# Attention and two expert layers on one core: pair products with the rows stationary, and the column softmax of two batches moved

## The chip, the core and the metric

The kernel runs on one core of a Trainium2 chip. The metric is the device time of one execution in microseconds (us), lower is better; three executions of the kernel before took 1196.97, 1197.18 and 1197.57 us. The engines are named as in the profile: PE (TensorE, with PEld for its weight loads), DVE (VectorE), ACT (ScalarE), POOL (GpSimd) and SP (the queue that issues most DMAs).

## The reference, cut to what matters

Three layers follow each other: an attention between 512 tokens and 32 state rows per head in both directions, a dense feed-forward layer, and a routed one in which each row goes to one of eight experts.

```python
def _attn_ref(x, state):                      # x 8 x 8 x 512 x 64, state 8 x 8 x 32 x 64
    scores = scale * np.matmul(x, state.transpose(0, 1, 3, 2))
    ...                                        # softmax over the 32 states
    xread = np.matmul(a, state)
    scores2 = scale * np.matmul(state, x.transpose(0, 1, 3, 2))
    ...                                        # softmax over the 512 tokens
    sread = np.matmul(a2, x)
    return np.concatenate([xread, sread], axis=2)

def _moe_ref(x, w_in, w_out):                 # w_in 512 x 2048, w_out 2048 x 512
    h = x @ w_in
    g = h * np.clip(h + 3.0, 0.0, 6.0) / 6.0
    return g @ w_out

def _moe2_ref(x, w_gate, w_output_gate, w1, w2):  # 8 experts, 512 x 1024 and 1024 x 512
    e_idx = np.argmax(x @ w_gate, axis=1)
    ...
    for e in range(E):
        h = np.maximum(x[mask] @ w1[e], 0.0)
        out[mask] = gate_w[mask, None] * eom[mask, e, None] * (h @ w2[e])
```

## The kernel before

**Dense part.** `w_in` and `w_out` arrive as 64-bit words. `from_f64` (L446) loads a tile of 512 such words per partition, has ACT scale the high words to 32 bits (L462), and has DVE shift the low words (L463), merge the sign bit into them (L464) and merge both (L465). `load_win(f)` and `load_wout(f)` do that for the 16 tiles of each matrix; the second also splits its tile into a rounded part and a rest (L474, L475), since products are made as three reduced-precision products. The raw tiles share four buffers (tag `x4`) with the loads of x.

For a batch, `attn_rows` (L177) makes the scores of all heads (`halves`, L163: eight products into two PSUM tiles), transposes them on DVE, and takes the softmax over the 32 states. Its inner `columns()` (L188) takes maxima (L192, L193) and exponentials (L194) of the same scores over the 512 tokens; for batch 0 it runs later and keeps batch 0's scores in the PSUM tiles o0 and o1 until then. `attn_cols` turns the exponentials and multiplies them with x. `make_sw` multiplies states and `w_in` (one call for four tiles of `w_in`), `h_xread` (L292) makes one tile `ft` of the hidden layer, `act` its activation, and `gemm2` (L332 to L334) the second product, two tiles later.

The order of the work at the start is a table, `plan`: for batch 0 and 1 and each tile `ft` it says which weight tiles are loaded and which steps of the generators `rows[b]`, `cols[b]` and `sws` are issued. Segments run batch 0's tiles 0 to 7, batch 1, batch 0's tiles 8 to 15, then batches 2 to 7. The scheduler reorders by priority; `soon(b)` raises that of batch 0 and 1.

**Routed part.** `ORDER` lists 19 slots: 16 slots of 256 rows of one expert (`gemm1` L682, `gemm2e` L698 to L702) and, as slots 5, 10 and 15 (counted from 0), a pair: 64 rows of each of two experts, in full precision. `pair1` (L654) is called for each of 8 tiles `ft`: w1's 128 x 128 blocks are the stationary operand, the 64 rows of each expert move. `pair2` (L665) then has the hidden values (64 columns per expert) stationary and w2's 512 columns moving, the two experts in two column tiles of the array at once. `slot` delays the second product by one tile, so PE's queue alternates the two. `finish` (L704) scales the result on ACT and scatters the rows by an indirect DMA on POOL; such a scatter waits until the one before has landed. Further pairs, behind `used`, are not executed with these data.

In PE's queue, a full-precision product is two instructions.

Of the kernel before, what the change touches and what calls it, by code (L numbers as in the profile page):

```python
# [80 lines left out]
def tile_kernel(  # L81
# [62 lines left out]


# [31 lines left out]
    def attn_rows(b):  # L177

        x = [loads.pop((b, k)) for k in range(2)]

        ps = halves(b, lambda j: x[j // 2][:, j % 2, :], ("o0", "o1") if b == 0 else None)
        sm = ap.tile([128, 72], F32, tag="sm", name="sm")
        mx, nm, s2, r2 = [sm[:, 2 * k:2 * k + 2] for k in range(4)]
        mr, sr, rr = [sm[:, k:k + 32] for k in (8, 40, 8)]
        bt = ap.tile([128, 32, NS], F32, tag="t4", name="bt", bufs=2)

        def columns():

            e2_t[b] = [win[3][:, e, :] for e in range(2)] if b == 0 else \
                [ap.tile([128, 512], F32, tag="e2", name="e2", bufs=2) for _ in range(2)], s2, r2  # L190
            for e in range(2):
                V.tensor_reduce(mx[:, e:e + 1], ps[e], axis=AX.X, op=ALU.max)  # L192
                V.tensor_scalar(nm[:, e:e + 1], mx[:, e:e + 1], -0.125, None, op0=ALU.mult)  # L193
                S.activation(e2_t[b][0][e], ps[e], AF.Exp, bias=nm[:, e:e + 1], scale=0.125,  # L194
                             accum_out=s2[:, e:e + 1])

        with soon(b):
            for e in range(2):
                V.transpose(bt[:, 16 * e:16 * e + 16, :].rearrange("p a n -> p (a n)"), ps[e])
            if b:  # L200
                columns()
        yield
        with soon(b):
            V.tensor_reduce(mr, bt, axis=AX.X, op=ALU.max)
        yield
        with soon(b):
# [3 lines left out]
        with soon(b):  # L210
# [4 lines left out]
        with soon(b):  # L215
# [7 lines left out]
        with soon(b):  # L223
            V.tensor_tensor(al, af, ah.bitcast(F32), op=ALU.subtract)
        aT[b] = ah, al
        yield
        if b == 0:
            columns()
            yield

    def attn_cols(b):

        e2, s2, r2 = e2_t.pop(b)
# [214 lines left out]
    def from_f64(src, dst=None):  # L448
# [14 lines left out]
        V.tensor_scalar(lw, lw, 29, None, op0=ALU.logical_shift_right)  # L463
        V.scalar_tensor_tensor(lw, y3.bitcast(U32), 0x80000000, lw, op0=ALU.bitwise_and, op1=ALU.bitwise_or)  # L464
# [3 lines left out]
    def load_win(f):  # L468
        o = 128 * (f % 4)
        from_f64(w_in[:, :, 256 * f:256 * f + 256], win[f // 4][:, :, o:o + 128])  # L470

    def load_wout(f):
        t = from_f64(w_out[:, f:f + 1, :])
        S.copy(woh[f], t)  # L474
        V.tensor_tensor(wol[f], t, woh[f].bitcast(F32), op=ALU.subtract)  # L475
# [177 lines left out]
    def pair1(ft, x):  # L653

        ps = psum("h", 2)[:, :128]
        for i in range(2):
            a = ws[2 + i][0][ft // 2][:, :, 128 * (ft % 2):128 * (ft % 2) + 128]
            for k in range(4):
                T.matmul(ps[:, 64 * i:64 * i + 64], a[:, k, :], x[:, k, 64 * i:64 * i + 64], start=(k == 0),  # L659
                         stop=(k == 3))  # L660
        hf = qa["p"].tile([128, 128], F32, tag="hf", name="hf", bufs=3)
        S.activation(hf, ps, AF.Relu)
        return ft, hf

    def pair2(py, ft, hf):  # L665
        for i in range(2):
            o = slice(64 * i, 64 * i + 64)
            T.matmul(py[0][o, :], hf[:, o], ws[2 + i][1][ft // 2][:, ft % 2, :], start=(ft == 0), stop=(ft == 7),  # L668
                     tile_position=(0, 64 * i))
# [34 lines left out]
    def finish(py, ids, gw, rows):  # L704
        for t in range(len(py)):
            y = mp.tile([128, DM], F32, tag="xr", name="y", bufs=4)
            S.activation(y, py[t], AF.Copy, scale=gw[:, t:t + 1])
            G.indirect_dma_start(rows, bass.IndirectOffsetOnAxis(ap=ids[:, t:t + 1], axis=0), y, None)
# [82 lines left out]
    def O(f):  # L791
        return lambda: load_wout(f)

    plan = {
        (0, 0): [I(2), go(sws[0, 0]), O(0)],
        (0, 1): [I(3), go(sws[0, 0]), O(1)],
        (0, 2): [go(rows[0]), I(4), go(sws[0, 1]), O(2), lambda: x_loads(1)],
        (0, 3): [I(5), go(sws[0, 1]), O(3)],
        (0, 4): [I(6), go(sws[0, 1]), O(4), go(rows[1])],
        (0, 5): [I(7), go(sws[0, 1]), O(5), go(rows[1], 2)],  # L800
        (0, 6): [O(6), go(rows[1], 2)],
        (0, 7): [O(7), go(rows[1]), lambda: q_loads(0)],
        (1, 0): [I(8), consts_in, go(cols[0], 2)],
        (1, 1): [I(9), go(cols[0], 2)],
        (1, 2): [I(10), go(cols[0])],
        (1, 3): [I(11)],
        (1, 4): [I(12), more_start],
        (1, 5): [O(8)],
        (1, 6): [I(13), O(9)],
        (1, 7): [I(14), O(10)],  # L810
        (1, 8): [I(15), O(11)],
        (1, 9): [O(12)],
        (1, 10): [O(13)],
        (1, 11): [O(14)],
        (1, 12): [O(15), lambda: q_loads(1)],
        (1, 13): [go(cols[1], 2)],
        (1, 14): [go(cols[1], 2)],
        (1, 15): [go(cols[1])],
# [88 lines left out]
    def drain(n):  # L907
        while len(pend) > n:
            s, py, args = pend.pop(0)
            (gemm2e if len(args) > 2 else pair2)(py, *args)  # L910
            if args[0] == 7:
                ids, _ = got.pop(s)
                finish(py, ids, turned.pop(s)[2], out[0:NX, :] if ORDER[s][0] == "1" else out)

    banks = [2]

    def slot(s):
        k, j = ORDER[s]
        py = []
        for t in range(1 if k == "p" else 2):  # L920
            py.append(f"o{banks[0] % 4}")
            banks[0] += 1
        last = s + 1 in stops
        for ft in range(8):
# [3 lines left out]
            args = pair1(ft, xh) if k == "p" else gemm1(big.index(s) % 2, ft, xh, xl)  # L928
            if ft == 0:
                drain(1)  # L930
                py = [psum(t) for t in py]
# [9 lines left out]
            if 0 < s < first and ft == 1 and ORDER[s - 1][0] == "p":  # L941
                fetch_pair(ORDER[s - 1][1] + 1)
            if ft == 1 and s + 2 < first:
                fetch_rows(s + 2)
            if ft == 4 and not last:
                turned[s + 1] = turn(got[s + 1][1])
        if k != "p":
            fetch_weights(big.index(s) + 2)
        if last:
            drain(0)  # L950
            if k == "p" and j + 1 < NP:
                fetch_pair(j + 1)

    first = NA + CUT
    stops = range(first, len(ORDER) + 1)
    for s in range(first):
        slot(s)
    used = nc.values_load(lists["used"][0:1, 0:1], min_val=0, max_val=NU)
    nest = ExitStack()
    for s in range(first, len(ORDER)):  # L960
        nest.enter_context(tc.If(used > 2 * ORDER[s][1]))
        fetch_rows(s)
        slot(s)
# [39 lines left out]
```

## Time and profile before

| | |
|---|---|
| median of three executions | 1197.18 us (1196.97 to 1197.57) |
| the profiled execution | 1196.95 us |
| its span, first to last instruction | 1195.2 us |
| PE busy | 1153.7 us (97%), 7160 instructions |
| DVE, ACT, POOL busy | 698.9 us (58%), 541.7 us (45%), 137.6 us (12%) |
| mean granted clock of TensorE | 0.988 |

Read the chain first: which engine's work ended last, and with what share. Then the stretches in which that engine idles or has a lower clock, by windows and its timeline, and what released it there. Stages differ: the first 70 us are not like the rest.

### The profile page before, as it was taken

Reading aid. Unit: us, or ns where it says so; the run is one execution under the profiler, and the core shown is the slowest. Engines: PE = TensorE matmul, PEld = TensorE weight load, DVE = VectorE, ACT = ScalarE, POOL = GpSimd, SP = SyncE. Lnnn points to the kernel's source line nnn. Section 1 sums busy time; section 2 is a strip of 40 time slices with the busy share of each in tenths; the row PEclk is TensorE's granted clock in tenths of the full one; section 3 lists DMA queues with packets and bytes.
Section 4 is the critical chain, followed back from the end, with each engine's and each line's share of the span. In section 5 each row is a group of like instructions: output and inputs, shape, how many; then the busy total and the mean of one; then the engine's idle time right before and its main releaser. Section 6 shows DMA issues by size and latency. Waiting matters only on the chain.

```text
span 1195.2 us, 19039 instructions
## 1 busy us (share of the span) xinstructions
PE 1153.7 (97%) x7160; PEld 902.3 (75%) x7160; DVE 698.9 (58%) x1473; ACT 541.7 (45%) x1039; POOL 137.6 (12%) x172
## 2 busy tenths in 40 slices
PE   4779999999999999999999999999999999999996
PEld 2547776677676677776777888899879988988895
DVE  6899657734735736547345475966436633663463
ACT  3465434333433434334333345566436644663463
POOL 0000001010000100100101013322222212131101
PEclk7989999999999999999999999999999999999998
DMA  5447214220210111110101029194175647811411
GB/s 180 152 163 219 90 62 84 70 60 15 71 38 29 45 37 36 39 36 1 37 1 36 1 46 323 46 347 175 54 271 202 239 167 279 340 45 36 147 40 38
DMA packets 53698, 128.35 MB, mean 107 GB/s; under 512 B 6736, under 2 KB 24400, under 8 KB 53584
## 3 DMA queue, kind: packets, MB, share of 16 engines
q1 hardware_dynamic: 46304, 108.66, 27.9%
q0 software_dynamic: 7296, 18.41, 4.3%
q8 instruction: 58, 0.95, 0.4%
q14 instruction: 40, 0.33, 0.1%
HBM read 145.36 MB, written 19.57 MB: 138 GB/s over the span
## 4 chain that ended last, share of the span: by engine, by line
PE 94%; DVE 3%; DMA 2%; ACT 0%; issue 0%; SPq 0%; POOL 0%; POOLq 0%; ACTq 0%; DVEq 0%
PE h L682 15%; PE h L292 15%; PE o L332 11%; PE o L333 11%; PE o L334 10%; PE o L698 5%; PE o L701 5%; PE o L702 5%; PE misc L173 5%; PE h L659 4%; PE o L668 2%; PE h L306 2%; PE misc L642 1%; PE misc L364 1%; DMA wo<-w_in 1%; PE misc L370 1%
## 5 line engine op out<-in xcount | busy, mean ns | idle before, releaser
L333 PE MATMUL o<-wol,gh 128*128 128x512 f32 x512 | 204.1, 399 | 1.5 <-DVE sm L193 1.1
L332 PE MATMUL o<-woh,gh 128*128 128x512 f32 x512 | 203.6, 400 | 0.2 <-ACT woh L474 0.2
L334 PE MATMUL o<-woh,gl 128*128 128x512 f32 x512 | 203.0, 397 | 0.0
L324 DVE SCALAR_TENSOR_TENSOR g<-r,h 128x512 f32<-128x512 f32 x128 | 87.7, 685 | 133.2 <-ACT r L323 133.1
L688 DVE TENSOR_TENSOR vl<-w2s,vh 128x512 fp32r<-128x512 f32 x128 | 88.6, 692 | 106.8 <-ACT vh L687 91.0
L323 ACT ACTIVATE r<-h 128x512 f32<-128x512 f32 x128 | 76.5, 598 | 156.6 <-PE h L292 156.2
L687 ACT CAST vh<-w2s 128x512 fp32r<-128x512 f32 x128 | 79.6, 622 | 102.0 <-PE o L702 101.1
L332 PEld LDWEIGHTS o<-woh,gh 128*128 128x128 f32 x512 | 96.0, 188 | 34.9 <-issue 12.5
L678 DVE TENSOR_TENSOR wl<-w1s,wh 128x512 fp32r<-128x512 f32 x128 | 88.7, 693 | 56.2 <-ACT wh L677 54.8
L326 DVE TENSOR_TENSOR gl<-g,gh 128x512 fp32r<-128x512 f32 x128 | 88.3, 690 | 54.0 <-ACT gh L325 53.8
L333 PEld LDWEIGHTS o<-wol,gh 128*128 128x128 f32 x512 | 96.0, 188 | 30.4 <-issue 5.9
L334 PEld LDWEIGHTS o<-woh,gl 128*128 128x128 f32 x512 | 96.0, 188 | 26.2 <-issue 4.4
L325 ACT CAST gh<-g 128x512 fp32r<-128x512 f32 x128 | 79.3, 619 | 76.7 <-DVE g L324 74.4
L438 POOL DMA_INDIRECT tab<-toku,ldsti x34 | 34.5, 1014 | 683.2 <-DVE ldsti L433 617.2
L292 PE MATMUL h<-ah,sh 128*128 128x512 f32 x256 | 108.5, 424 | 1.6 <-ACT sh L279 1.6
L292 PE MATMUL h<-al,sh 128*128 128x512 f32 x256 | 102.3, 400 | 0.0
L292 PE MATMUL h<-ah,sl 128*128 128x512 f32 x256 | 101.6, 398 | 0.1
L702 PE MATMUL o<-vh,hl 128*128 128x512 f32 x256 | 101.4, 396 | 0.0
L701 PE MATMUL o<-vl,hh 128*128 128x512 f32 x256 | 101.1, 395 | 0.0
L677 ACT CAST wh<-w1s 128x512 fp32r<-128x512 f32 x128 | 79.7, 623 | 41.9 <-PE h L682 40.4
L682 PEld LDWEIGHTS h<-xh,wh 128*128 128x128 f32 x512 | 76.4, 188 | 15.9 <-issue 4.9
L682 PE MATMUL h<-xh,wh 128*128 128x256 f32 x512 | 83.2, 284 | 1.3 <-ACT xh L647 1.3
(196 smaller groups left out, 1876.7 us busy)
## 6 DMA issues: line engine op xcount, KB each, us to landing
w1s<-w SPq DMA_DIRECT2D x96, 512.0 KB
w2s<-w SPq DMA_DIRECT2D x96, 512.0 KB
xd<-xr SPq DMA_DIRECT2D x34, 256.5 KB
xT<-xT SPq DMA_DIRECT2D x16, 512.0 KB
wo<-w_in SPq DMA_DIRECT2D x16, 512.0 KB
wo<-w_out SPq DMA_DIRECT2D x16, 512.0 KB
xq<-xq SPq DMA_DIRECT2D x16, 512.0 KB
half<-xp SPq DMA_DIRECT2D x4, 256.0 KB
```

What stands on the lines that cost most here:

```text
L292: T.matmul(ps, w[:, o:o + 128], a[:, e, :], start=(n == 0), stop=(n == 5))
L324: V.scalar_tensor_tensor(g6, r, 6.0, ps, op0=ALU.min, op1=ALU.mult)
L326: V.tensor_tensor(gl, g6, gh.bitcast(F32), op=ALU.subtract)
L332: T.matmul(po[t], gh[:, s], woh[ft], start=first, stop=False)
L333: T.matmul(po[t], gh[:, s], wol[ft], start=False, stop=False)
L334: T.matmul(po[t], gl[:, s], woh[ft], start=False, stop=last)
L677: S.copy(wh, a)
L678: V.tensor_tensor(wl, a, wh.bitcast(F32), op=ALU.subtract)
L682: T.matmul(ps, w[:, k, :], x[:, k, :], start=(m == 0), stop=(m == 11))
L688: V.tensor_tensor(vl, c, vh.bitcast(F32), op=ALU.subtract)
L701: T.matmul(py[t], hh[:, sl], vl, start=False, stop=False)
L702: T.matmul(py[t], hl[:, sl], vh, start=False, stop=(ft == 7))
```

## The change

Seven edits; the core of the diff stands below.

1. The products of a pair: `pair1` now has an expert's 64 rows stationary, for each 128 of the 512 inputs, and w1's columns moving, 256 at a time, the two experts in two column tiles. The result lies with rows on partitions, so `pair_relu` (ACT) and `pair_turn` (four PE transposes and a copy on DVE, for each half of the hidden layer) bring it into the form that `pair2` takes. A pair is one function `pair(s)`, no longer interleaved with itself tile by tile.
2. `columns` leaves `attn_rows`. For batch 0 and 1, `attn_cols` loads x again, makes the scores again (`halves`) and takes the exponentials; in `plan` it moves from tile 2 of batch 0 and tiles 0 to 2 of batch 1 to tiles 9 to 15 of batch 1, with the loads `X` and `Q`.
3. `rows[1]` is issued over tiles 3 to 7 of batch 0, without raised priority (`soon0`).
4. For the `w_out` tiles 1 to 15 and the `w_in` tiles 10 to 15, ACT makes the sign word (Sign, then Relu with scale -2^31), and DVE merges shift and sign in one instruction.
5. Some loads of `w_in` and `w_out` change place in `plan`.
6. `finish` declares its scatters independent of each other; they wait for those of the slot before.
7. In the last of the 19 slots, the second of the two scalings is on DVE.

```diff
-    def from_f64(src, dst=None):
+    def from_f64(src, dst=None, sign=False):
...
-        V.tensor_scalar(lw, lw, 29, None, op0=ALU.logical_shift_right)
-        V.scalar_tensor_tensor(lw, y3.bitcast(U32), 0x80000000, lw, op0=ALU.bitwise_and, op1=ALU.bitwise_or)
+        if sign:
+            S.activation(hw.bitcast(F32), y3, AF.Sign)
+            S.activation(hw, hw.bitcast(F32), AF.Relu, scale=-2.0 ** 31)
+            V.scalar_tensor_tensor(lw, lw, 29, hw, op0=ALU.logical_shift_right, op1=ALU.bitwise_or)
+        else:
...
+    def attn_cols(b):
+        if b < 2:
+            x = [loads.pop((b, k)) for k in range(2)]
+            columns(b, halves(b, lambda j: x[j // 2][:, j % 2, :]))
             yield
...
+    def pair1(ps, c, x):
+        for k in range(4):
+            for i in range(2):
+                o = slice(64 * i, 64 * i + 64)
+                T.matmul(ps[o, 256 * (c % 2):256 * (c % 2) + 256], x[:, k, o], ws[2 + i][0][c][:, k, :],
+                         start=(k == 0), stop=(k == 3), tile_position=(0, 64 * i))
...
+    def pair_turn(h):
+        ps = psum("misc", 2)
+        for k in range(4):
+            T.transpose(ps[:, 128 * k:128 * k + 128], h[:, 128 * k:128 * k + 128], ident)
+        hT = mp.tile([128, 4, 128], F32, tag="gl", name="hT", bufs=3)
+        V.tensor_copy(hT.rearrange("p k t -> p (k t)"), ps)
+        return hT
...
+            if quick and t:
+                V.tensor_scalar(y, py[t], gw[:, t:t + 1], None, op0=ALU.mult)
+            else:
+                S.activation(y, py[t], AF.Copy, scale=gw[:, t:t + 1])
+            i = G.indirect_dma_start(rows, bass.IndirectOffsetOnAxis(ap=ids[:, t:t + 1], axis=0), y, None).ins
+            for o in new:
+                tc.declare_no_dep(i, o, reason="a row is in one place")
+            after(i, written)
+            new.append(i)
...
-        (0, 2): [go(rows[0]), I(4), go(sws[0, 1]), O(2), lambda: x_loads(1)],
+        (0, 2): [I(4), go(sws[0, 1]), O(2), X(1)],
...
+    def pair(s):
...
+        pair1(ps, 0, x)
+        drain(0)
+        pair1(ps, 1, x)
+        h = [pair_relu(ps)]
...
+        pair1(ps, 2, x)
+        hT = [pair_turn(h[0])]
+        pair1(ps, 3, x)
+        h.append(pair_relu(ps))
+        py = bank()
+        for ft in range(8):
+            if ft == 2:
+                hT.append(pair_turn(h[1]))
+            if ft == 4 and s + 1 < first:
+                turned[s + 1] = turn(got[s + 1][1])
+            pair2(py, ft, hT[ft // 4])
```

How the order of instructions changes, at the three places of which the prediction speaks. The rows are the order of each engine's queue; how long something takes is not in them.

PE, in the first pair, before: L659 are `pair1`'s products (two rows of four for a tile), L668 are `pair2`'s (one row for each expert).

```order
L668 MATMUL o_8627<-w2s_6897,hf 64x512
L668 MATMUL o_8627<-w2s_6905,hf 64x512
L659 MATMUL h<-xf,w1s_6894 128x64 x4
L659 MATMUL h<-xf,w1s_6902 128x64 x4
L668 MATMUL o_8627<-w2s_6897,hf 64x512
L668 MATMUL o_8627<-w2s_6905,hf 64x512
```

And now, at the passage from the first to the second products: L669 is `pair1`, L680 a turn of half of the hidden layer, L688 `pair2`.

```order
L669 MATMUL h<-w1s_6955,xf 64x256
L669 MATMUL h<-w1s_6963,xf 64x256
L688 MATMUL o_8738<-w2s_6956,hT 64x512
L688 MATMUL o_8738<-w2s_6964,hT 64x512
L688 MATMUL o_8738<-w2s_6956,hT 64x512
L688 MATMUL o_8738<-w2s_6964,hT 64x512
L680 MATMUL misc<-ident,hr 128x128 x4
L688 MATMUL o_8738<-w2s_6957,hT 64x512
L688 MATMUL o_8738<-w2s_6965,hT 64x512
```

The alternation after every tile is gone: 32 first products come in four blocks of eight (before the third and the fourth, and after the first, other products stand), the first turn stands between the third and the fourth block, the second turn behind two tiles of second products.

DVE, in batch 0's tiles 1 and 2, before: L463, L464 and L465 convert a weight tile, L192 and L193 belong to batch 0's column softmax, L475 is the rest of a `w_out` tile.

```order
L463 TENSOR_SCALAR wo<-wo 128x512
L326 TENSOR_TENSOR gl<-g_311,gh 128x512
L464 SCALAR_TENSOR_TENSOR wo<-wy,wo 128x512
L280 TENSOR_TENSOR sl_0_0_163<-misc,sh_0_0_162 128x128
L280 TENSOR_TENSOR sl_0_1_165<-misc,sh_0_1_164 128x128
L465 SCALAR_TENSOR_TENSOR wz<-wy,wo 128x512
L192 TENSOR_REDUCE sm<-o_145 128x1
L192 TENSOR_REDUCE sm<-o_146 128x1
L324 SCALAR_TENSOR_TENSOR g_389<-r,h 128x512
L475 TENSOR_TENSOR wol_104<-wz,woh_88 128x512
L193 TENSOR_SCALAR sm<-sm 128x1 x2
L463 TENSOR_SCALAR wo<-wo 128x512 x2
```

And now the same place: L474 to L476 are the three old steps of a conversion, L472 the merged step of a `w_out` tile.

```order
L472 SCALAR_TENSOR_TENSOR wo<-wo 128x512
L331 TENSOR_TENSOR gl<-g_312,gh 128x512
L285 TENSOR_TENSOR sl_0_0_163<-misc,sh_0_0_162 128x128
L285 TENSOR_TENSOR sl_0_1_165<-misc,sh_0_1_164 128x128
L476 SCALAR_TENSOR_TENSOR wz<-wy,wo 128x512
L474 TENSOR_SCALAR wo<-wo 128x512
L475 SCALAR_TENSOR_TENSOR wo<-wy,wo 128x512
L486 TENSOR_TENSOR wol_104<-wz,woh_88 128x512
L329 SCALAR_TENSOR_TENSOR g_385<-r,h 128x512
L476 SCALAR_TENSOR_TENSOR win_120<-wy,wo 128x4x128
```

The maxima and their scaling are gone from here, and the `w_out` tile takes L472 and L476 alone.

POOL, the end of the last slots, before, with what each scatter waits for (DMASW: the landing of an earlier DMA of this queue; Activation or DVE: the scaling):

```order
L708 DMA out<-y,ids 4480x512 [waits DMASW6_49,Activation_49]
L708 DMA out<-y,ids 4480x512 [waits DMASW7_49,Activation_49]
L708 DMA out<-y,ids 4480x512 [waits DMASW0_49,Activation_49]
L708 DMA out<-y,ids 4480x512 [waits DMASW1_49,Activation_49]
L958 TENSOR_LOAD used [waits DVE_49]
```

And now:

```order
L735 DMA out<-y,ids 4480x512 [waits DMASW6_49,DMASW5_49,Activation_49]
L735 DMA out<-y,ids 4480x512 [waits Activation_49]
L735 DMA out<-y,ids 4480x512 [waits DMASW7_49,DMASW0_49,Activation_49]
L735 DMA out<-y,ids 4480x512 [waits DVE_49]
L1016 TENSOR_LOAD used [waits DVE_49]
```

Before, each scatter waits for a landing; now the second of a slot waits for its own data alone, at the end for DVE.

## Rows read from the trace of the kernel before

**Rows 1.** The page, part 4: the chain that ended last, by engine.

```profile
PE 94%; DVE 3%; DMA 2%; ACT 0%; issue 0%; SPq 0%; POOL 0%; POOLq 0%; ACTq 0%; DVEq 0%
```

**Rows 2.** Windows: busy time and clock; a start-up stretch and the first pair's.

```profile
core 0: us, PE busy (x) PEld busy (x) DVE busy (x) ACT busy (x) POOL busy (x), PEclk, DMA share, GB/s
22.05:67.66 45.61, 32.71 (x214) 20.91 (x213) 39.55 (x79) 23.58 (x51) 0.00 (x0) 0.91 0.42 139
...
855.99:883.06 27.07, 27.07 (x187) 19.71 (x185) 3.40 (x7) 6.58 (x16) 5.23 (x7) 1.00 0.43 141
```

**Rows 3.** Timeline of PE, start-up: start, length, what, [idle before <- releaser].

```profile
46.95 0.45 PE L173 MATMUL misc<-win,st 64*32 64x128 f32 x16 [1.15 <-DVE win L465]
...
66.47 0.80 PE L173 MATMUL misc<-win,st 64*32 64x128 f32 x16 [6.32 <-DVE sm L212]
```

**Rows 4.** Timeline of DVE, start-up.

```profile
31.93 0.44 DVE L463 TENSOR_SCALAR wo<-wo 128x512 uint32<-128x512 uint32 x1
32.26 0.68 DVE L326 TENSOR_TENSOR gl<-g,gh 128x512 fp32r<-128x512 f32 x1
32.87 0.68 DVE L464 SCALAR_TENSOR_TENSOR wo<-wy,wo 128x512 uint32<-128x512 uint32 x1
...
34.47 1.28 DVE L192 TENSOR_REDUCE sm<-o 128x1 f32<-128x512 f32 x2
```

**Rows 5.** Lines by form: ScalarE's exponentials of the column softmax.

```profile
L194 ACT ACTIVATE e<-misc,sm 128x512 f32<-128x512 f32 x14 | 9.6, 686 | 19.8 <-DVE sm L193 19.6
```

**Rows 6.** Waits of SP's queue, 0 to 130 us: total us, times, longest.

```profile
SPq L452 <- DVE win L465: 41.8, 13, 5.9
```

**Rows 7.** Timeline of PE, the first pair.

```profile
857.69 0.71 PE L698 MATMUL o<-vh,hh 128*128 128x512 f32 x2
...
859.17 1.89 PE L659 MATMUL h<-xf,w1s 128*128 128x64 f32 x16
...
862.00 2.00 PE L659 MATMUL h<-xf,w1s 128*128 128x64 f32 x16
863.93 1.08 PE L668 MATMUL o<-w2s,hf 128*64 128x512 f32 x4
864.94 2.00 PE L659 MATMUL h<-xf,w1s 128*128 128x64 f32 x16
...
870.81 1.09 PE L642 MATMUL misc<-ident,xg 128*128 128x128 f32 x8
871.74 1.90 PE L659 MATMUL h<-xf,w1s 128*128 128x64 f32 x16
...
880.45 0.74 PE L682 MATMUL h<-xh,wh 128*128 128x256 f32 x4
...
882.05 1.08 PE L668 MATMUL o<-w2s,hf 128*64 128x512 f32 x4
```

**Rows 8.** Windows of line L668 alone, slices of 0.05 us in one group.

```profile
860.95:861.00 0.05, 0.01 (x2) 0.01 (x2) 1.00 0.00 0
...
861.40:861.45 0.05, 0.05 (x2) 0.00 (x0) 1.00 1.61 164
861.45:861.50 0.05, 0.05 (x4) 0.00 (x0) 1.00 0.40 164
```

**Rows 9.** Timelines: one group's weight loads; elsewhere four column tiles of 256 columns.

```profile
863.92 0.20 PEld L668 LDWEIGHTS o<-w2s,hf 128*64 128x64 f32 x4
...
312.41 0.64 PE L370 MATMUL misc<-x2T,wg_sb 128*32 128x256 f32 x8
```

**Rows 10.** Lines by form: a copy out of PSUM on DVE.

```profile
L365 DVE COPY x2T<-misc 128x512 f32<-128x512 f32 x34 | 23.2, 688 | 8.9 <-PE misc L364 8.9
```

**Rows 11.** Timeline of PE: one batch's scores.

```profile
55.15 1.09 PE L173 MATMUL misc<-xT,st 64*32 64x512 f32 x16
```

**Rows 12.** Timeline, the end of the run: the last two row scatters.

```profile
1185.58 0.96 POOL L708 DMA_INDIRECT out<-y,ids  x1 [16.56 <-ACT y L707]
1189.17 0.96 POOL L708 DMA_INDIRECT out<-y,ids  x1 [2.64 <-DMA out<-y,ids]
```

More of the change, by code (lines that the diff above doesn't have):

```diff
@@ L651, in turn, with pair_relu, pair2 @@
         return xh, xl, gw
[L653 to L665, printed above, removed]
+    def pair1(ps, c, x):
[4 more added lines that the diff above has]
+                         start=(k == 0), stop=(k == 3), tile_position=(0, 64 * i))
+    def pair_relu(ps):
+        h = mp.tile([128, 512], F32, tag="gh", name="hr", bufs=3)
+        S.activation(h, ps, AF.Relu)
+        return h
+    def pair_turn(h):
[5 more added lines that the diff above has]
+        return hT
+    def pair2(py, ft, hT):
         for i in range(2):
             o = slice(64 * i, 64 * i + 64)
[L668 to L669 removed]
+            T.matmul(py[o, :], hT[:, ft % 4, o], ws[2 + i][1][ft // 2][:, ft % 2, :], start=(ft == 0),
+                     stop=(ft == 7), tile_position=(0, 64 * i))
     def gemm1(i, ft, xh, xl):
@@ L792, in O, with X, Q @@
         return lambda: load_wout(f)
+    def X(b):
+        return lambda: x_loads(b)
+    def Q(b):
+        return lambda: q_loads(b)
     plan = {
@@ L909, in drain, with bank @@
             s, py, args = pend.pop(0)
-            (gemm2e if len(args) > 2 else pair2)(py, *args)
+            gemm2e(py, *args)
             if args[0] == 7:
                 ids, _ = got.pop(s)
-                finish(py, ids, turned.pop(s)[2], out[0:NX, :] if ORDER[s][0] == "1" else out)
+                finish(py, ids, turned.pop(s)[2], out[0:NX, :] if ORDER[s][0] == "1" else out, s + 1 == first)
     banks = [2]
+    def bank():
+        banks[0] += 1
+        return psum(f"o{(banks[0] - 1) % 4}")
     def slot(s):
[L918 to L923, printed above, removed]
+        g = big.index(s)
         for ft in range(8):
@@ L940, in slot @@
                 fetch_pair(0)
-            if 0 < s < first and ft == 1 and ORDER[s - 1][0] == "p":
-                fetch_pair(ORDER[s - 1][1] + 1)
             if ft == 1 and s + 2 < first:
                 fetch_rows(s + 2)
-            if ft == 4 and not last:
+            if ft == 4 and s + 1 < first:
                 turned[s + 1] = turn(got[s + 1][1])
[L947 to L952, printed above, removed]
+        fetch_weights(g + 2)
+    def pair(s):
+        j = ORDER[s][1]
+        if s not in turned:
+            turned[s] = turn(got[s][1])
+        x, _, gw = turned.pop(s)
+        ps = psum("h", 2)
+        pair1(ps, 0, x)
+        drain(0)
+        pair1(ps, 1, x)
+        h = [pair_relu(ps)]
+        if s + 2 < first:
+            fetch_rows(s + 2)
+        ps = psum("h", 2)
+        pair1(ps, 2, x)
[6 more added lines that the diff above has]
+                hT.append(pair_turn(h[1]))
+            if ft == 4 and s + 1 < first:
+                turned[s + 1] = turn(got[s + 1][1])
+            pair2(py, ft, hT[ft // 4])
+        finish([py], got.pop(s)[0], gw, out)
+        if j + 1 < NP:
+            fetch_pair(j + 1)
     first = NA + CUT
-    stops = range(first, len(ORDER) + 1)
     for s in range(first):
-        slot(s)
+        (pair if ORDER[s][0] == "p" else slot)(s)
+    drain(0)
     used = nc.values_load(lists["used"][0:1, 0:1], min_val=0, max_val=NU)
@@ L962, in tile_kernel @@
         fetch_rows(s)
-        slot(s)
+        pair(s)
     nest.close()
```

92 lines of the change are left out of this document (47 added, 45 removed).

## The prediction

> **What bounds the kernel now.** I read the chain first: PE holds 94% of it, DVE 3%, DMA 2% [rows 1]. So what PE need not do shortens the run, unless PE then waits. Next the windows by stage [rows 2]. In the first pair's stretch of 27.07 us PE is busy for all of it at a clock of 1.00, DVE for 3.40 and ACT for 6.58 us: PE alone sets the pace. From 22.05 to 67.66 us it is different: PE is busy for 32.71 of 45.61 us, DVE for 39.55; PE's 12.90 us of idle time are DVE's. PE's timeline there [rows 3] shows the longest gap, 6.32 us, released by DVE. Behind it the same sixteen products take 0.80 us that took 0.45 before: the clock had fallen to its lower level during the gap. So a pair is to be costed on PE's timeline, the start on DVE's, the end on the last scatters.
>
> **The pairs' products.** One pair before: the stretch of 27.07 us, less what is not the pair's. That is 859.17 - 857.69 = 1.48 us and 882.05 - 880.45 = 1.60 us of the neighbouring slots, and 871.74 - 870.81 = 0.93 us of eight transposes for the next slot, which stay [rows 2, 7]. 27.07 - 4.01 = 23.06 us. In it sixteen groups alternate: of first products, 863.93 - 862.00 = 1.93 us each, and of second ones, 864.94 - 863.93 = 1.01 us each [rows 7].
>
> After the change both kinds have 64 rows stationary and two experts in two column tiles. How fast that runs, L668 shows already. Its group of four instructions begins at 860.99 us (0.01 us busy in the slice to 861.00) with two instructions; two more join in the slice from 861.45 [rows 8]. So two column tiles of 512 columns run at once, and the next two follow after 0.46 us. A group of 1.01 us is two such sets and 0.09 us of entry. From that:
> - First products: 32 products are 64 instructions, 32 sets. With 256 columns I take half of 0.46, 0.23 us. 32 x 0.23 = 7.36, and four entries of 0.09: 7.72 us.
> - Second products: 16 sets of 512 columns as now, 7.36, and three entries, since turns now split them twice: 7.63 us.
> - Eight new transposes of 128 x 128: 0.93 us, the price of the eight in [rows 7].
>
> Together 16.28 us, 6.78 less than 23.06; three pairs **20.3 us**. The bounds: without any entry 7.41 a pair, 22.2. At the other end stands the nearest row with 256 columns: two sets of four column tiles in 0.64 us, 0.32 a set [rows 9]; 32 x 0.09 = 2.88 more, 3.9 a pair, 11.7. I take 0.23, because that row is one short group with its entry and its end in it, while L668 shows the distance from one set to the next.
>
> One thing could make it wrong: weight loads, which now come every 0.23 us instead of 0.46. The four loads of an L668 group start with the group and are over in 0.20 us [rows 9], while the first set runs for 0.46 [rows 8]; so the second set's loads passed beside running products, at 0.05 us a load or 0.10 a set. The Trainium skill, "TensorE: Matmul & The Clock Gate", Part 3, "The mechanism", says otherwise: a weight load overlaps running products only where it goes to other row groups, and these use all rows. The trace disagrees, as far as four loads go. By the rule each set would cost 0.23 + 0.10 us, rival B.
>
> The ReLU (a pass like the exponentials of 0.686 us [rows 5]) and the copy of the turned half (0.688 us [rows 10]) cost nothing, if covered. In PE's new order a block of eight first products (8 sets, 1.84 us) stands between the first ReLU and its turn, another between that turn and the second products; the second ReLU has two tiles (four sets, 1.84 us) before its turn, the second copy two more. ACT and DVE are mostly idle there [rows 2]. Without that cover up to 2 x (0.69 + 0.69) = 2.75 us a pair would show: rival A.
>
> **The end.** Scatter one is issued from 1185.58 to 1186.54, scatter two at 1189.17, 2.64 us of idle time behind it for the landing of the first [rows 12]. In the new order it waits for DVE's scaling alone, which runs beside ACT's. It can go at about 1186.8: I take **2.3 us**. Bounds: 2.63 if it follows at once, 0 if two scatters in flight take as long as one after the other, of which the trace has no case. The other slots' scatters are covered by PE's work.
>
> **The start.** From DVE's queue in the stretch go four maxima, two pairs of 1.28 us [rows 4]: 2.56. For the `w_out` tiles 1 to 7, which lie there, one merge takes the place of a shift and a merge. The shift's step is 32.26 - 31.93 = 0.33 us, that of a two-operand pass 32.87 - 32.26 = 0.61 [rows 4]; the merged one also has two operands, so 0.33 a tile go, 7 x 0.33 = 2.31. DVE is the bound there, so PE's idle time shrinks by 4.87. Later PE makes two batches' scores again: 2 x 1.09 = 2.18 us [rows 11], in a stage in which nothing but PE binds, so that all of it counts. The maxima and exponentials lie there beside PE's work; if a later step waited for them, that would be in rival C. If the long gap shortens, the slow products behind it return 0.80 - 0.45 = 0.35 us [rows 3]. Net 4.87 - 2.18 + 0.35 = **3.0 us**. At best all idle time goes: 12.90 - 2.18 = 10.7 us.
>
> ACT pays: 14 passes of about 0.69 us for seven tiles, 9.6 us, less four exponentials, 2.7 [rows 5]; 23.58 becomes 30.5 of 45.61 us, not a bound as a sum. But the merge is now behind two ACT passes, 1.37 us, in an ACT queue that works in order behind the loads, and the activations of the hidden tiles and state's rounding stand behind them. The raw tile keeps its buffer for that long, and SP's loads already wait 41.8 us in all, 13 times, for DVE to free one [rows 6]: rival C. The other moved loads bring the same bytes, plus x of two batches again, at a DMA share of 0.42 [rows 2]; I cost them at nothing while DMA has that room.
>
> **Sum.** The profiled run took 1196.95 us (span 1195.2 and 1.75 around it), 0.23 below the median of the runs. 1196.95 - 20.3 - 2.3 - 3.0 = **1171.4 us**.
>
> **The rivals.**
> - A, the pair's ReLU and turn show (0.07): 3 x 2.75 = 8.3 back, 1179.7. For it: ACT and DVE work in order, the neighbours' work ahead of these steps. Against: 3.40 and 6.58 us of work in 27 [rows 2].
> - B, weight loads don't overlap (0.06): 32 x 0.10 x 3 = 9.6 back, 1181.0. Against it [rows 8, 9], for a set twice as long.
> - C, the start gives its gain back (0.15): between nothing won, 1174.4, and all of the 9.6 us of ACT's passes falling on the chain: 5.2 won, 9.6 and 2.18 lost, a net loss of 6.6, so 1181.0. For it: loads that wait for buffers [rows 6], and ACT's queue is in order. Against: four buffers, and ACT a third idle.
> - E, the start wins far more (0.08): the gaps are waits in chains, and taking maxima out of them lets loads start sooner. All idle time gone: 7.7 more, 1163.7.
> - D, the other side (0.03): the clock falls in the pairs. At half clock a pair takes 32.6 us, 9.5 more than before; 28.5 less the 5.3 of end and start is 23.2 us slower, 1220. It decides from a pair of 23.06 + 5.3 / 3 = 24.8 us on, a mean granted clock there below 0.66. For it: PE has this lower level and fell to it after 6.32 us of idle time [rows 3], and a pair with stalls has idle time. Against: the stretch with L668 and eight transposes ran at 1.00 without idle time [rows 2, 7], and no gap like that is in sight. The Trainium skill, same page, Part 4 "PE-mode transpose", says that transposes don't count like other products for releasing the clock. By it eight more of them a pair make D likelier; the trace shows no fall at the eight it has.
>
> That the change doesn't do what it says I rule out by the order: the alternation is gone, the scatter waits for its data alone, the maxima have left.
>
> **How the numbers follow.** The forecast has 0.60, the rivals 0.39, no measurable difference 0.01 (the gains would have to cancel by chance). The range, 1163 to 1182, takes in A, B, C and E, and the bounds of the single terms one at a time; D and several mishaps together are left out. Two tenths of a per cent, 2.4 us, is about what a measurement can tell from no change. Every case but D lies more than that below 1197: faster 0.96, same 0.01, slower 0.03.
>
> **What would show it.** Right: blocks of sixteen L669 instructions of 1.8 to 2.0 us; L688 tiles 0.92 apart; a pair near 16.3 us at clock 1.00 without idle time, L680 waiting for nothing; the last two scatters some 1.3 us apart; PE's idle time from 22 to 68 us near 8 us instead of 12.9. Wrong: L669 sets of 0.3 us or more (B), idle time at L680 or behind it (A), a granted clock under 1 in a pair (D), waits for `w_out` merges on Sign and Relu and no less idle time at the start (C), or hardly any (E).

## The result, and the profile after

The changed kernel takes 1179.09 us (median of four runs, 1178.41 to 1180.76); the kernel before took 1197.38 us beside it. The ratio is 0.9848, with a 95% interval of 0.9831 to 0.9865. So it is faster by some 18 us; the forecast was 1171.4, with a range of 1163 to 1182. The profiled execution took 1178.88 us, its span is 1177.0, 18.2 less than before.

Three points on the timelines split these 18.2 us. The last product of the whole run starts at 1167.17 instead of 1184.60. The layer behind the dense one starts with its first product here (timeline of PE, kernel before and then the change):

```profile
682.06 0.64 PE L306 MATMUL h<-x1h,wih 128*128 128x256 f32 x4
```

```profile
686.49 0.63 PE L311 MATMUL h<-x1h,wih 128*128 128x256 f32 x4
```

Up to there the change is **4.43 us late**, where 3.0 us of gain had been forecast. From there to the last product it takes 480.68 instead of 502.54 us, 21.86 less: that is the pairs (three times the 7.35 us found below are 22.05). From the last product to the end it takes 9.83 instead of 10.60 us.

**The pairs.** Timeline of PE, first pair of the change (L669 first products, L680 turns, L688 second products):

```profile
860.51 1.95 PE L669 MATMUL h<-w1s,xf 128*64 128x256 f32 x16
862.39 0.73 PE L718 MATMUL o<-vh,hh 128*128 128x512 f32 x2
...
863.98 3.67 PE L669 MATMUL h<-w1s,xf 128*64 128x256 f32 x32
867.59 0.66 PE L680 MATMUL misc<-ident,hr 128*128 128x128 f32 x4
868.17 1.95 PE L669 MATMUL h<-w1s,xf 128*64 128x256 f32 x16
869.95 1.89 PE L688 MATMUL o<-w2s,hT 128*64 128x512 f32 x8
871.77 0.66 PE L680 MATMUL misc<-ident,hr 128*128 128x128 f32 x4
872.35 1.94 PE L688 MATMUL o<-w2s,hT 128*64 128x512 f32 x8
874.22 1.09 PE L653 MATMUL misc<-ident,xg 128*128 128x128 f32 x8
875.24 3.65 PE L688 MATMUL o<-w2s,hT 128*64 128x512 f32 x16
878.83 0.74 PE L702 MATMUL h<-xh,wh 128*128 128x256 f32 x4
```

No row has idle time. Read by starts: 32 instructions of L669 from 863.98 to 867.59, 3.61 us, are sixteen sets of 0.226 us, as the half of [rows 8] had it. First products 1.88 + 3.61 + 1.78 = 7.27 us (forecast 7.72), turns 2 x 0.58 = 1.16 (0.93), second products 1.82 + 1.87 + 3.59 = 7.28 (7.63): a pair is 15.71 us, not 16.28. Windows of the same kernel, the pair and the place of the next part (columns as in [rows 2]):

```profile
860.51:878.83 18.32, 18.32 (x120) 9.18 (x119) 5.35 (x8) 6.30 (x11) 4.95 (x5) 1.00 0.69 216
...
22.00:68.00 46.00, 40.55 (x251) 23.94 (x250) 39.25 (x71) 33.06 (x64) 0.00 (x0) 0.91 0.52 161
68.00:90.00 22.00, 21.17 (x90) 15.24 (x90) 19.34 (x34) 13.75 (x24) 0.00 (x0) 1.00 0.59 175
90.00:130.00 40.00, 38.06 (x218) 26.74 (x217) 30.77 (x52) 32.94 (x62) 0.00 (x0) 0.96 0.59 177
122.00:124.00 2.00, 2.00 (x16) 0.22 (x14) 1.03 (x3) 1.97 (x5) 0.00 (x0) 0.61 0.69 258
124.00:126.00 2.00, 2.00 (x11) 1.40 (x5) 0.95 (x2) 1.74 (x4) 0.00 (x0) 0.54 0.02 6
```

**The start.** PE's idle time from 22 to 68 us fell from 12.9 [rows 2] to 5.45 us. But a new hole opens at 119.8 us, and behind it the clock is near its lower level for some 4 us (0.61 and 0.54). In the kernel before, PE had been full in this stage:

```profile
90.00:130.00 40.00, 40.00 (x195) 30.44 (x196) 37.94 (x70) 24.34 (x43) 0.00 (x0) 1.00 0.70 215
```

Timelines of the change around the hole, PE, ACT and DVE:

```profile
115.72 1.09 PE L176 MATMUL misc<-xT,st 64*32 64x512 f32 x16
...
119.41 0.39 PE L339 MATMUL o<-woh,gl 128*128 128x512 f32 x1
121.74 2.62 PE L176 MATMUL misc<-win,st 64*32 64x512 f32 x16 [1.94 <-ACT e L229]
```

```profile
113.71 0.66 ACT L468 ACTIVATE wy<-wo 128x512 f32<-128x512 f32 x1 [1.05 <-DMA wo<-w_out]
...
115.49 0.68 ACT L471 ACTIVATE wo<-wo 128x512 uint32<-128x512 f32 x1
...
120.91 0.69 ACT L229 ACTIVATE e<-misc,sc 128x512 f32<-128x512 f32 x1 [1.52 <-DVE sc L228]
```

```profile
116.21 0.70 DVE L472 SCALAR_TENSOR_TENSOR wo<-wo 128x512 uint32<-128x512 uint32 x1 [0.61 <-ACT wo L471]
116.94 0.69 DVE L476 SCALAR_TENSOR_TENSOR wz<-wy,wo 128x512 uint32<-128x512 uint32 x1
...
119.53 1.28 DVE L227 TENSOR_REDUCE sc<-misc 128x1 f32<-128x512 f32 x2
120.73 0.27 DVE L228 TENSOR_SCALAR sc<-sc 128x1 f32<-128x1 f32 x2
```

Read backwards: `make_sw`'s products at 121.74 need a `misc` PSUM buffer. Both hold the second scores of batch 0 (PE at 115.72) until the exponentials (L229) have read them. These wait for the maxima (L227), which start at 119.53, 2.7 us after the scores: in DVE's queue they stand behind the conversion of a `w_out` tile (L472, L476, then g, wol and gl). That conversion waited for ACT's sign word (L471), and ACT for a late load. Sixteen of these instructions take 1.09 us at full clock; they took 2.62. With 0.2335 us from one product of the dense part to the next, as elsewhere in this stage, PE loses 4.4 us between 118 and 127 us (an estimate: from 118.24 to 126.97, less fourteen products at that pace and 1.09 us for the sixteen).

### The profile page after: what moved, and what is told of

Read it like the earlier page. It is cut to its first block, busy times and chain, and to the rows that moved or that the text cites. A ratio compares the mean times of both kernels' runs of the same rounds, so it can differ in the third digit from the quotient of the medians.

```text
span 1177.0 us, 18771 instructions
## 1 busy us (share of the span) xinstructions
PE 1140.7 (97%) x7024; PEld 875.4 (74%) x7024; DVE 699.9 (59%) x1459; ACT 561.5 (48%) x1062; POOL 134.6 (11%) x172
## 4 chain that ended last, share of the span: by engine, by line
PE 91%; ACT 3%; DVE 2%; DMA 2%; issue 1%; POOL 0%; SPq 0%; ACTq 0%; POOLq 0%
PE h L702 15%; PE h L297 14%; PE o L337 10%; PE o L338 10%; PE o L339 10%; PE o L718 5%; PE o L721 5%; PE o L722 5%; PE misc L176 5%; PE h L311 2%; PE h L669 2%; PE o L688 2%; PE misc L653 1%; PE misc L369 1%; DMA wo<-w_out 1%; PE misc L375 1%
## 5 line engine op out<-in xcount | busy, mean ns | idle before, releaser
L337 PE MATMUL o<-woh,gh 128*128 128x512 f32 x512 | 202.9, 403 | 2.2 <-ACT woh L485 2.1
L339 PE MATMUL o<-woh,gl 128*128 128x512 f32 x512 | 203.8, 398 | 0.0
L337 PEld LDWEIGHTS o<-woh,gh 128*128 128x128 f32 x512 | 96.1, 189 | 39.5 <-issue 15.0
L339 PEld LDWEIGHTS o<-woh,gl 128*128 128x128 f32 x512 | 96.3, 188 | 27.0 <-issue 4.4
L297 PE MATMUL h<-ah,sh 128*128 128x512 f32 x256 | 108.9, 426 | 1.8 <-ACT sh L284 1.8
L297 PE MATMUL h<-ah,sl 128*128 128x512 f32 x256 | 102.6, 401 | 0.1
L297 PE MATMUL h<-al,sh 128*128 128x512 f32 x256 | 102.4, 400 | 0.0
L722 PE MATMUL o<-vh,hl 128*128 128x512 f32 x256 | 101.5, 396 | 0.0
```

Of the source, the lines that this page charges most:

```text
L297: T.matmul(ps, w[:, o:o + 128], a[:, e, :], start=(n == 0), stop=(n == 5))
L337: T.matmul(po[t], gh[:, s], woh[ft], start=first, stop=False)
L339: T.matmul(po[t], gl[:, s], woh[ft], start=False, stop=last)
L722: T.matmul(py[t], hl[:, sl], vh, start=False, stop=(ft == 7))
```

## The experiments

All times are against the kernel before on the same chip. The first eight kernels ran where its median was 1198.3 to 1199.1 us. The last four (cols_first, mixed, half_cols, late_no_sign) ran where it took 1202.4; there each kernel has 1.9 to 2.6 us of idle time near 200 us that the others lack, so these are compared by their ratio, or within one profile; whether the kernel before idles there too on that chip, no profile shows. The edits are cut to their core (`...`), and stand against the change unless the text names another kernel.

**old_start**: the start of before (columns at the old place, no Sign, old plan), with the new pairs and end.

```diff
-        if b < 2:
-            x = [loads.pop((b, k)) for k in range(2)]
-            columns(b, halves(b, lambda j: x[j // 2][:, j % 2, :]))
...
-        (1, 9): [O(12), go(cols[0]), Q(0)],
+        (1, 9): [O(12)],
...
```

> The change's pairs and its end, with the start of the kernel before: column softmax at its old place, no Sign, the old order of loads. Theory L (late columns): by the two traces the pairs give 21.9 us and the end 0.8, and the new start costs 4.4 us by the first row of the dense part's last stage. So this kernel takes 1197.4 - 22.7 = 1174.7 us (1173.5 to 1176), faster than the change by some 4.4. Theory S (sign chain) expects the same here. If the start were no loss and the pairs gave less than the trace says, it would take 1179 or more.

1174.4 us, ratio 0.9796 (0.9782 to 0.9809). As expected: the pairs and the end carry the whole gain, and the new start takes some of it back.

**sign_only** and **no_sign** split the start: old_start with Sign for the same tiles as the change, and the change without Sign.

```diff
-        t = from_f64(w_out[:, f:f + 1, :])
+        t = from_f64(w_out[:, f:f + 1, :], None, f > 0)
...
```

```diff
     def from_f64(src, dst=None, sign=False):
+        sign = False
```

> As old_start, with the sign words by ScalarE for the same tiles as in the change, and nothing else of the start. Theory L: Sign takes 0.33 us a tile from DVE in a stretch where DVE sets the pace, so this gains, up to 2.3 us: 1172.5 to 1174.7. Theory S: the two ScalarE passes lengthen the way of a raw tile and hold its buffer, so most of the loss of 4.4 us stands here: 1177.5 to 1179.

> The change, without the sign words by ScalarE (all tiles converted in the old three steps by DVE). Theory L: recomputed scores (2.0 us), the wait at batch 1's late columns and the slower clock behind it (some 4.4 us) stay, and DVE has more to do: 1179 to 1182. Theory S: the loss goes with the passes: 1172 to 1175.

sign_only: 1175.51 us, 0.9802 (0.9788 to 0.9815). no_sign: 1176.26 us, 0.9812 (0.9799 to 0.9826). Neither theory got both: Sign alone neither wins nor costs, the moved columns alone cost little, and only together they cost. That last step rests on the profiles, where the layer behind the dense one starts at 683.78 us in no_sign and at 685.61 and 686.49 in two executions of the change; of the ratios, no_sign's interval lies outside the change's first (0.9831 to 0.9865), but overlaps that of its second run (0.9821 to 0.9848). And Sign does not show in PE's idle time of the first stretch. It is the same without it as in the change (window of no_sign):

```profile
22.00:68.00 46.00, 40.59 (x252) 25.55 (x252) 41.78 (x78) 25.51 (x51) 0.00 (x0) 0.92 0.50 161
```

In sign_only the waits have changed places: PE now waits 4.55 us for `wol` (timeline of PE):

```profile
63.23 0.79 PE L333 MATMUL o<-wol,gh 128*128 128x512 f32 x1 [4.55 <-DVE wol L481]
```

In no_sign the maxima start as soon as the scores are there (DVE's timeline), and PE's products take 1.76 instead of 2.62 us, with no idle time ahead of them (PE's):

```profile
117.43 1.29 DVE L227 TENSOR_REDUCE sc<-misc 128x1 f32<-128x512 f32 x2 [0.65 <-PE misc L176]
```

```profile
120.32 1.76 PE L176 MATMUL misc<-win,st 64*32 64x512 f32 x16
```

**cols1_later**: batch 1's columns behind `make_sw` of the same tile.

```diff
-        (1, 13): [go(cols[1]), Q(1)],
-        (1, 14): [go(cols[1], 2)],
-        (1, 15): [go(cols[1], 3)],
-        (0, 8): [load_part],
+        (1, 13): [Q(1)],
+        (1, 14): [go(cols[1])],
+        (1, 15): [go(cols[1], 2)],
+        (0, 8): [load_part, go(cols[1], 3)],
```

> The change, with batch 1's column softmax one tile later, so that the products of states and w_in for the next segment (which took a PSUM buffer that the columns' scores held) come first. Theory L: the wait of 1.94 us and the slow clock behind it, together 4.45 us over the nominal pace between 118 and 127 us, go: 1174 to 1176. Theory S: nothing of the sign words changes, so 1178 to 1180.

1177.21 us, 0.9813 (0.9800 to 0.9827), between the two ranges, and the wait is still there:

```profile
121.50 2.52 PE L176 MATMUL misc<-win,st 64*32 64x512 f32 x16 [1.91 <-ACT e L229]
```

So the step was wrong: the scores that block there are batch 0's, whose states stand in those instructions. It led to the next run.

**after_again** and **both_later**: the change as a yardstick, and both batches' columns behind `make_sw` (batch 0's steps move from tiles 9 to 12 to tiles 10 to 13).

```diff
-        (1, 9): [O(12), go(cols[0]), Q(0)],
-        (1, 10): [O(13), go(cols[0], 2)],
+        (1, 9): [O(12), Q(0)],
+        (1, 10): [O(13), go(cols[0])],
...
```

> The change itself, on the same chip as the next three, as their yardstick: 1178.5 to 1180.5 us, with the wait of about 1.9 us near 121 us again.

> The change with batch 0's column softmax one tile later, and batch 1's one tile later too, so that each batch's recomputed scores come behind the products of states and w_in of the same tile. cols1_later kept the wait at 121.5 us: the scores that held the PSUM buffers there were batch 0's (its states' tile stands in the rows), not batch 1's. If that wait and the slow clock behind it are the bulk of the start's loss, they go now: 4.45 us less than the change, and up to 1 more for batch 1's, so 1173.5 to 1175.5. If they only hid another limit (late w_out tiles and the ScalarE passes), the gain is under 2 us: 1177 or more, with waits on L485 or L476 in their place.

after_again: 1178.18 us, 0.9834 (0.9821 to 0.9848), with a wait of 1.62 us, but this time the clock stays at 1.00 behind it (122.10 to 126 us), and the layer behind the dense one starts at 685.61 (PE's timeline):

```profile
122.14 1.75 PE L176 MATMUL misc<-win,st 64*32 64x512 f32 x16 [1.62 <-ACT e L229]
```

both_later: 1177.19 us, 0.9825 (0.9811 to 0.9838); the wait is gone, with the order of the two kinds of products turned round (PE's timeline):

```profile
115.15 1.09 PE L176 MATMUL misc<-win,st 64*32 64x512 f32 x16
...
120.56 1.09 PE L176 MATMUL misc<-xT,st 64*32 64x512 f32 x16
```

In the profile the start gets 1.9 to 2.8 us shorter (683.67 against 685.61 and 686.49); it was the quickest of its five executions, 1175.82 us. The time moved by less than its interval, so as a time this run is inconclusive, and the 4.45 us that were expected are not there.

**sign_early** and **late_no_sign**: sign words for `w_out` tiles 1 to 7 alone (and for no tile of `w_in`), with the columns behind, and with the columns at the change's places.

```diff
-        t = from_f64(w_out[:, f:f + 1, :], None, f > 0)
+        t = from_f64(w_out[:, f:f + 1, :], None, 0 < f < 8)
...
```

> As both_later, with the sign words by ScalarE for w_out tiles 1 to 7 alone, those that fall into the stretch where DVE sets the pace. Late in batch 1 neither engine sets the pace, so Sign can only lengthen the chain there. If Sign pays in the first stretch and costs later: 1172 to 1174. If the chain of ScalarE's passes costs in the first stretch too (sign_only gained nothing there), no better than both_later: 1174 to 1176.

> The change with the sign words by ScalarE for w_out tiles 1 to 7 alone; the columns stay at the change's places. It completes a square: change (late sign words, columns at tile 9), both_later (late sign words, columns behind), sign_early (none, columns behind). In DVE's queue batch 0's maxima still stand behind w_out tile conversions here. If the wait near 121 us needs the ScalarE passes in those conversions (DVE's merge waited for them, and they for a late load), it is under 0.3 us or gone, as in no_sign, and the time over that of the kernel before is at 0.980 to 0.9825. If the order alone makes it, 1.5 to 2 us of wait on L229 stay and the ratio is 0.983 or more.

sign_early: 1174.77 us, 0.9806 (0.9792 to 0.9819). late_no_sign: 0.9817 (0.9796 to 0.9838), too wide to tell much. Its profile says more: the maxima start at 117.40, there is no wait ahead of `make_sw`, and its products take as long as in no_sign; behind them PE waits 0.72 us for DVE's L285 (DVE's timeline, then PE's):

```profile
117.40 1.29 DVE L227 TENSOR_REDUCE sc<-misc 128x1 f32<-128x512 f32 x2
```

```profile
120.29 1.76 PE L176 MATMUL misc<-win,st 64*32 64x512 f32 x16
```

So the wait at 121 us needs ACT's two passes in the conversion ahead of the maxima, and the scores ahead of `make_sw` in PE's queue (both_later has the passes, but `make_sw` first). The late load alone doesn't make it: ACT waits for it in all of these, 1.05 us in the change, 1.09 in both_later, 0.78 in no_sign and 0.89 in late_no_sign. With the passes the merge comes 2.50 us after ACT has begun with the tile (113.71 and 116.21 in the change), without them 0.72 (113.20 and 113.92 in late_no_sign). That the maxima's place in DVE's queue is the link is read from DVE's rows; the run that was to test it is the next one.

**cols_first**: raised priority for the second scores and their columns.

```diff
+            with tc.high_priority(400):
-            columns(b, halves(b, lambda j: x[j // 2][:, j % 2, :]))
+                columns(b, halves(b, lambda j: x[j // 2][:, j % 2, :]))
```

> The change, with raised priority for the recomputed scores, maxima and exponentials of batch 0 and 1. Nothing moves in the plan, but the scheduler puts batch 0's maxima on DVE ahead of two w_out conversions that stood before them, and its scores on PE some 50 instructions before the products of states and w_in instead of 14. If the wait near 121 us is DVE's queue order (maxima behind conversions that wait for ScalarE's sign words and a late load), it goes here as in both_later: the first product of the layer behind batch 7 (686.5 in the change's trace, 683.7 in both_later) comes at 683.5 to 684.5 us, the time is 1176 to 1177.5. If PSUM's two buffers are too few for the scores wherever they stand, a wait on an exponential (L229, here L230) stays, and with it 686 us and 1178.

0.9883 (0.9860 to 0.9907), slower than the change and outside both forecasts. The priority moved the scores on PE too, ahead of where their x could be loaded:

```profile
108.80 1.93 PE L176 MATMUL misc<-xT,st 64*32 64x512 f32 x8 [4.60 <-DVE wo L473]
```

x shares its four buffers with the raw tiles, which are free behind their last merge (L477 in this kernel): SP's loads of the two halves of x waited 2.3 and 3.8 us for it and were issued at 103.96 and 108.16 us. The row names L473, the DVE step that ended last; that PE waited for x is read from these loads. The maxima start at 115.60 here, as soon as the scores are there, and `make_sw` at 124.98 waits for no exponential (1.09 us). But the scores now stand 10.5 us ahead of `make_sw`, so the run doesn't separate the two orders, DVE's and PE's; it shows the price of putting a product into PE's queue before its input.

**mixed**: sign_early with batch 0's columns at the old place, from the kept scores (edit against sign_early).

```diff
-        if b < 2:
+        if b == 1:
...
-        (0, 2): [I(4), go(sws[0, 1]), O(2), X(1)],
+        (0, 2): [go(rows[0]), I(4), go(sws[0, 1]), O(2), X(1)],
...
```

> As sign_early, but batch 0's column softmax at its old place, from the scores kept in o0 and o1 (no second scores for it); batch 1's as in sign_early. By the step of the prediction that prices the start by DVE's time: 1.28 us of maxima come back to a stretch that DVE bounds, 1.02 us of scores leave a stretch that PE bounds; so no difference beyond 1 us from sign_early, 1174 to 1176. If it is the second scores and the PSUM that they hold that cost, rather than DVE's time: 1172 to 1173.5.

0.9809 (0.9797 to 0.9822), no difference from sign_early's 0.9806: DVE's time in the first stretch and PE's time later weigh about the same.

**serial_end**: old_start with the scatters in series (edit against old_start).

```diff
-            for o in new:
-                tc.declare_no_dep(i, o, reason="a row is in one place")
-            after(i, written)
-            new.append(i)
-        written[:] = new
```

> As old_start, with the row scatters in series again (each waits for the landing of the one before); the last scaling stays on DVE. By the traces, two scatters in flight brought the end of the span 0.8 us nearer to the last product, not 2.3, since the second took longer to land (4.5 instead of 2.9 us in the median). So from the last product to the end 10.0 to 10.3 us here, against 9.4 with the change; time 1175 to 1176.5. If the 1.5 us that are missing were an accident of one profile, the distance is 11.5 to 12.

1176.8 us, 0.9818 (0.9803 to 0.9833). From the last product to the end of the span it takes 11.28 us (1163.72 to 1175.0), between the two distances that were forecast. In the twelve profiles with two scatters in flight this distance lies between 8.7 and 10.0 us, 9.3 in the median; before it was 10.6. The last line of the end's DMA issues, in the kernel before and in the change, shows what was given back (count, median us to landing):

```profile
out<-y,ids POOLq DMA_INDIRECT x2, 2.9
```

```profile
out<-y,ids POOLq DMA_INDIRECT x2, 4.5
```

The 4.5 is the second scatter's landing alone; that of the first isn't in the change's trace. In the eight profiles that show it, the second of two in flight lands after 3.7 to 4.7 us; one at a time they took 2.8 to 3.4 (before and serial_end).

**half_cols**: sign_early, with w1's columns 128 at a time (edit against sign_early).

```diff
-                T.matmul(ps[o, 256 * (c % 2):256 * (c % 2) + 256], x[:, k, o], ws[2 + i][0][c][:, k, :],
+                    q = 256 * (c % 2) + 128 * n
+                    T.matmul(ps[o, q:q + 128], x[:, k, o], ws[2 + i][0][c][:, k, 128 * n:128 * n + 128],
...
```

> As sign_early, with w1's columns moving 128 at a time instead of 256 in a pair's first products: 128 instructions a pair instead of 64, of half the length, and a weight load for each. If weight loads pass beside running products in other row groups or not, as the L668 group of the kernel before shows (0.05 us a load, two for a set of 0.115 us), a pair stays as long, within 0.5 us. If a load has to wait for the products that run (rival B's rule), 64 sets cost 0.1 us each more than with 256 columns: 6 us a pair, 19 in all, and L669's sets come every 0.21 us instead of 0.115.

One execution, 1179.11 us where the kernel before took 1202.4 (0.981). Half the columns and twice the weight loads take the same time (timelines of PE and PEld):

```profile
864.06 3.71 PE L671 MATMUL h<-w1s,xf 128*64 128x128 f32 x64
```

```profile
864.06 3.47 PEld L671 LDWEIGHTS h<-w1s,xf 128*64 128x64 f32 x64 [0.37 <-issue]
```

64 instructions in 3.71 us, against 32 in 3.67 in the change: 32 sets of 0.115 us, with two weight loads in each. Rival B falls.

## Why the prediction was right, and where it was not

**The pairs: right, and a little small.** 20.3 us were forecast, 21.9 came. Both kinds of products ran at the pace read from [rows 8]; the 0.32 us a set of [rows 9] was rightly kept as a bound only. The entries were dearer by estimate than in fact, the turns cheaper (0.93 against 1.16 us). ReLU and copy are hidden (rival A falls), the clock is 1.00 in the pair in spite of sixteen transposes in that stretch (rival D falls), and half_cols shows that the loads pass beside running products. So the rule of the Trainium skill, "TensorE: Matmul & The Clock Gate", Part 3, "The mechanism", that a weight load overlaps running products only in other row groups, does not hold here for two column tiles of the same rows. The Trainium skill, same page, Part 4 "PE-mode transpose", says that transposes don't count like other products for releasing the clock; with the 1.00 above, that cost nothing in this kernel.

**The end: right in kind, too large.** 2.3 us were forecast; the median of twelve profiles gives 10.6 - 9.3 = 1.3, and against serial_end 2.0. The second scatter goes 1.27 us behind the first, as forecast, but lands later than one that is alone (3.7 to 4.7 us against 2.8 to 3.4). The lower bound of this term had named that case.

**The start: wrong in sign.** 3.0 us of gain were forecast, the profiles show 3.6 to 4.4 of loss. Its first step came near in size, but not by its terms. Of the dense part's products (L292 and L332 to L334, later L297 and L337 to L339), counted from the first one behind 21.9 us, which starts at 22.0 to 22.3, these are the times from that first one on; the last column is counted from the start of the span:

| | 301st | 325th | 501st product | layer behind starts |
|---|---|---|---|---|
| before | 101.0 | 106.7 | 156.5 us | 682.06 |
| old_start | 101.8 | 107.4 | 157.2 | 682.78 |
| sign_only | 101.5 | 107.1 | 157.0 | 682.45 |
| no_sign | 95.1 | 103.9 | 157.0 | 683.78 |
| both_later | 94.1 | 101.0 | 157.0 | 683.67 |
| sign_early | 94.6 | 101.5 | 155.7 | 682.57 |
| the change | 94.6 | 106.8 | 159.9 | 686.49 |
| after_again | 95.4 | 106.0 | 159.0 | 685.61 |
| late_no_sign | 95.1 | 104.8 | 157.8 | 687.92, with the idle time near 200 us |
| mixed | 98.4 | 104.1 | 154.9 | 685.57, with the idle time near 200 us |

At the 301st product the change leads by 6.5 us. Some 2.5 of them are batch 0's column products, which it still has to do (two L246 of 0.6, two L254 of 0.65 us). It has batch 0's second scores behind it, but not yet the fourth `make_sw` of the full width, which the kernel before has done; at 1.09 us each these cancel. That leaves about 4 us of true gain, against 4.87 + 0.35 forecast. No_sign, with the same work done by then, has 3.4 of the 4, and sign_only is 0.3 ahead of old_start. So Sign gave 0.3 to 0.6 us, within the noise, where 2.31 were forecast; the rest, 3.4, came with the columns and the loads and rows that moved with them, where 2.56 were forecast for the maxima. That the sum came out near is in part luck. The second scores cost 1.0 us each, as forecast. Old_start and before differ by 0.7 us with the same start: so much is noise.

**The step that failed is one sentence**: "The maxima and exponentials lie there beside PE's work". They cost some 5.4 us there: 3.36 us late at the 501st product is 4 us won, 2.0 us of second scores lost, and the rest. DVE and ACT were not busy enough for that (30.77 and 32.94 of the 40 us from 90 to 130); it was the order. PE's next products needed the PSUM that the scores held, with one tile of work between, and DVE's queue had a conversion in front of the maxima. Of the 5.4 us, 4.4 lie between 118 and 127 us, the wait of 1.94 and the slow clock behind it. That was in rival C's condition ("if a later step waited for them"), and its time, 1174.4 to 1181.0, holds the result. But its mechanism was put in the wrong place: raw tiles that hold their buffers in the first stretch. That part is not borne out, since sign_only with all its passes there costs nothing that can be measured. What Sign does is to lengthen the conversion ahead of the maxima at 116 us; without it there, the 501st product comes 2.1 us earlier (late_no_sign). The total lies in a range that was made wide by rivals whose mechanisms did not come as described; as far as the start goes, that is luck.

The total misses by 7.7 us: the start is 7.4 worse in the profiles shown (4.4 lost for 3.0 won), the end 1.5, the pairs 1.6 better, 0.2 is the run against its median and 0.1 the time around the span.

What stays open: both_later and sign_early take away the wait, but at the 501st product only 0.8 us of the early 4 are left in the better of them, sign_early, after 2.0 for the scores. Where the other 1.2 go, in short waits inside rows (make_sw's sixteen products in 1.75 us) or in the moved column steps, the runs do not settle. Behind the 501st product another 0.9 us are lost: 504.4 us to the next layer, against 503.5 before. The five others that moved both batches' columns and don't idle near 200 us take 504.5 to 504.6 there, and old_start, sign_only and serial_end 503.5, all with the same products and without idle time; no run says why. Nor is it shown why the clock fell behind a wait of 1.94 us (and, in cols1_later, 1.91: 0.67 and 0.56) and not behind one of 1.62.

The best version is **old_start**, 0.9796, with **sign_early** (0.9806) beside it: below the change (0.9834 and 0.9848), outside its intervals, and not apart from each other (nor from mixed, 0.9809, which is the furthest ahead at the 501st product). The pairs and the end alone are the better change.

## What to carry to other kernels

When work leaves a stage that DVE bounds for one that PE bounds, its own time can be the smaller part of the price: look at which PSUM buffer it holds, who needs that next on PE, and what stands in front of its steps in the queues of DVE and ACT. Of a matmul with few rows, make the rows stationary and let the long side move, two experts at once in column tiles: here a pair went from 23.1 to 15.7 us, and the pace could be read beforehand from another line of the same kernel. Price parts of a change by undoing them one at a time: two parts that cost little or nothing alone cost together.

## What the runs showed of the hardware

Two weight loads for every 0.115 us of products in two column tiles cost nothing that shows (half_cols: 3.71 us, against 3.67 with half as many loads in the change). Of two row scatters in flight the second landed after 3.7 to 4.7 us, one at a time after 2.8 to 3.4. ScalarE's Sign and Relu take 0.68 us each for 128 x 512 (near 115 us of the change), like the scaling ahead of them (0.66).
